# Retention attention feeding a gated MLP, on one core: scores of two heads on the two row halves of the PE array, and the running state kept as 64-column diagonal blocks

## The chip, the cores and the metric

The kernel runs on one core of a Trainium2 chip. The metric is the device time of one execution in microseconds (us); where several runs were made the median is given. "Granted clock" is the share of full TensorE clock that the throttle allowed. All profiles and ratios here are of fast runs; three of the 33 runs of the kernel before that stood beside the experiments were slow and are left out of the ratios.

Engines: PE multiplies matrices (PEld is its weight load, which overlaps), DVE is the vector engine, ACT the scalar engine, POOL the general one, SP issues the input DMAs.

## The reference, cut to what matters

```python
# q, k, v: (8 batches, 8 heads, 576 positions, 64), float32
scores = (q @ k.T) / sqrt(64)
ret = scores * Dmat              # Dmat[i, j] = gamma_h ** (i - j) for i >= j, else 0
x = (ret @ v)                    # heads side by side: (8, 576, 512)

h = gelu_tanh(x @ w_in)          # 512 -> 1024; u, v = its two halves
v_n = layer_norm(v) * g_ln
v_s = einsum('ts,bsd->btd', w_sg, v_n) + b_sg   # mixes positions
out = x + (u * v_s) @ w_out
```

## The kernel before

Two batches of 576 positions make nine tiles of 128 positions; four such periods make 36 tiles. The decay is folded into v and into a table, so a tile's attention is: scores with a triangular mask within the tile, plus a running state (64 x 64 per head) for everything earlier. Heads have 64 channels, so two heads fill 128 partitions. The kernel before multiplies a head pair at full array height by padding with zeros: `kbd` has the transposed k of one head in partitions 0 to 63 and zeros elsewhere, and so on; `zbd` is the state as a padded block-diagonal.

```python
    kbds = [consts.tile([128, KK, 2, 128], BF, ...) for i in range(2)]   # set to zero once
    zbds = [consts.tile([128, KK, 128], BF, ...) for i in range(2)]      # set to zero once

    def attn_T(i):            # transposes of k and q, and their way out of PSUM
        for a in (1, 0):
            for kk in range(KK):
                nc.tensor.transpose(tp[:, a, kk, :], s["qkb"][:, a, kk * 128:(kk + 1) * 128], ident[:])
        nc.scalar.activation(kbd[:64, :, 0, :], tp[:64, 1, :, :], Act.Copy)     # ACT: half of k
        nc.vector.tensor_copy(qT[:], tp[:, 0, :, :])                            # DVE: q
        nc.vector.tensor_copy(kbd[64:, :, 1, :], tp[64:, 1, :, :])              # DVE: other half of k

    def attn_S(i):            # scores, masked into ret
        for j in range(2):
            for r in range(4):
                kk, hh = 2 * j + r // 2, r % 2
                nc.tensor.matmul(sc[:, r, :], s["kbd"][:, kk, hh, :], s["qT"][:, kk, :], ...)
            nc.vector.tensor_tensor(ret[:, 4 * j:4 * j + 4, :], sc[:], msk..., op=Alu.mult)

    def attn_O(i):            # ot = state part + in-tile part; xT = ot * table
        ... nc.tensor.matmul(ot[r, kk, :n], st["zbd"][:, kk, r], s["qT"][:, kk, :n], ...)
        ... nc.tensor.matmul(ot[64 * hh:64 * hh + 64, kk, :], s["vp"][...], s["ret"][:, h, :], ...)
        nc.vector.tensor_tensor(xTs[p][...], ot[:], ttab[...], op=Alu.mult)

    def attn_Z(i):            # state update, and its copy for the next tile
        for kk in range(KK):
            nc.tensor.matmul(z[:, kk, :], kn[:, kk * 128:(kk + 1) * 128], s["vp"][:, kk * 128:(kk + 1) * 128], ...)
        nc.scalar.activation(zb[64:, :, 64:], z[64:, :, 64:], Act.Copy)         # ACT: half
        nc.vector.tensor_copy(zb[:64, :, 0:64], z[:64, :, 0:64])                # DVE: half

    for i in range(1, N + 1):           # ... loads, weight building and guards cut
        prep(i + 2)                     # POOL: casts of q, k, v
        attn_S(i)
        mlp_norm(i - 2)                 # ACT: vn = (vg - mean) * rstd
        run()                           # one queued unit: wp (mixing, then DVE gT) or op (output, then ACT ob)
        mlp_V(i - 1)                    # PE: hv; ACT: vg = gelu(hv)
        attn_T(i + 1)
        mlp_stats(i - 1)                # DVE: bst = bn_stats(vg)
        run()                           # another queued unit
        mlp_rstd(i - 1)                 # DVE: mv; POOL: rs, rs, nm
        mlp_U(i - 1)                    # PE: hu; ACT: uT
        attn_O(i); attn_Z(i)
```

So there are tiles with two wp units, tiles with two op units, and one tile per period with a single op unit (or none). They are called two-wp, two-op and one-op tiles below. The two-op tiles come in pairs; where one figure is given for them, it is that of the second of a pair.

## Time and profile before

| | before |
|---|---|
| time, median of 4 runs | 268.6 us (267.3 to 269.7) |
| span of the profiled execution, granted clock | 267.6 us, 0.973 |
| busy PE / DVE / ACT / POOL | 85 / 66 / 53 / 44% |
| tiles up to the start of the fifth xT | 46.1 us |
| the next 31 tiles (to the start of the last xT) | 199.2 us, 6.43 each |
| from there to the end | 22.3 us |

The first stage waits for DMA, the last is nearly all PE. (xT is the DVE product that ends a tile's attention; its start is a handy mark in the timeline.)

The first part of the page of the kernel before gives busy time, share and instructions of each engine:

```profile
PE 227.5 (85%) x2594; PEld 164.6 (62%) x2630; DVE 176.4 (66%) x394; ACT 143.1 (53%) x249; POOL 117.6 (44%) x202
```

The next lines are from its timeline: start, duration, engine, line, operation, outputs and inputs. They follow one loop through a tile with two op units; a bracket is idle time before the instruction and what ended it.

```profile
104.20 0.18 DVE L332 BATCH_NORM_AGGREGATE mv<-bst 128x2 f32<-128x6 f32 x1
...
105.82 0.82 ACT L349 ACTIVATE vn<-vg,nm,rs 128x512 bf16<-128x512 f32 x1 [1.46 <-POOL nm L337]
...
106.66 0.60 ACT L390 ACTIVATE ob<-op 128x512 f32<-128x512 f32 x1
...
107.67 0.60 ACT L322 ACTIVATE vg<-hv 128x512 f32<-128x512 f32 x1 [0.41 <-ACT ob L390]
108.16 0.58 ACT L254 ACTIVATE kbd_156<-tp 64x512 bf16<-64x512 bf16 x1
...
108.77 0.42 DVE L255 COPY qT<-tp 128x512 bf16<-128x512 bf16 x1 [2.15 <-ACT kbd_156 L254]
...
109.23 0.43 DVE L256 COPY kbd_156<-tp 64x512 bf16<-64x512 bf16 x1
...
109.69 0.69 DVE L327 BATCH_NORM_STATS2 bst<-vg 128x6 f32<-128x512 f32 x1
...
110.49 0.18 DVE L332 BATCH_NORM_AGGREGATE mv<-bst 128x2 f32<-128x6 f32 x1
```

Read it as a circle: the variance (mv) goes through three POOL steps (nm is the last; cut here) to the normalisation (vn) on ACT; ACT is in order, so ob, vg and the k copy stand behind vn; qT on DVE waits for ACT's k copy; the second half of k and bn_stats (bst) stand behind qT; then comes the next mv, 6.29 us after the first. That is exactly the time of a tile. PE in such a tile needs only 5.75 us (the sum of the distances between the starts of its groups), so it idles.

PE's groups for the attention, from the timeline of a tile with two wp units of the kernel before (x8 is the number of matmuls in the group; a group lasts until the next one starts):

```profile
122.90 0.41 PE L284 MATMUL ot<-qT,zbd_158 128*64 128x128 bf16 x8
123.15 0.39 PE L289 MATMUL ot<-ret,vsc_151 128*64 128x128 bf16 x8
123.47 0.40 PE L305 MATMUL zp<-vsc_151,qkb 128*128 128x128 bf16 x4
123.71 0.61 PE L267 MATMUL sc<-qT,kbd_156 128*128 128x128 bf16 x8
124.15 0.41 PE L372 MATMUL wp<-wT_0_178,vn 128*128 128x288 bf16 x2
```

From the first ot to wp is 1.25 us: state part 0.25, in-tile part 0.32, state update 0.24, scores 0.44.

### The profile page before, as it was taken

How to read it: one execution, taken by the hardware profiler on the slowest of the kernel's cores; microseconds unless marked ns; L12 is line 12 of the kernel's file. 1: busy time of each engine (PE TensorE's matmuls, PEld its weight loads, DVE VectorE, ACT ScalarE, POOL GpSimd, SP SyncE). 2: the span in 40 equal slices, each digit the busy share in tenths (PEclk: the TensorE clock that was granted, in tenths of full speed). 3: DMA queues.
4: the chain of work that ended last, by engine and by line, in shares of the span. 5: the costliest groups of instructions: out<-in, count | busy, mean ns of one | idle time of the engine just before them, and what ended most of it. 6: DMA issues, size and time to landing. Idle time of an engine off the chain costs nothing.

```text
span 267.6 us, 6555 instructions
## 1 busy us (share of the span) xinstructions
PE 227.5 (85%) x2594; PEld 164.6 (62%) x2630; DVE 176.4 (66%) x394; ACT 143.1 (53%) x249; POOL 117.6 (44%) x202
## 2 busy tenths in 40 slices
PE   0558669868999999969999999799999999799894
PEld 0337437646766776747766876468666766576552
DVE  4475667599856985568658866578669866575230
ACT  7274486763455446654465466624564466544513
POOL 7137642544455655535445444444446455311100
PEclk9999986999999999999999999979999999889999
DMA  8999996999527997599949968785683022000305
GB/s 150 247 283 202 273 271 148 226 212 220 99 81 198 194 218 181 163 248 182 199 134 223 219 144 212 186 155 107 142 218 80 2 80 81 39 2 0 133 26 196
DMA packets 120453, 42.64 MB, mean 159 GB/s; under 512 B 113700, under 2 KB 113700, under 8 KB 120424
## 3 DMA queue, kind: packets, MB, share of 16 engines
q1 hardware_dynamic: 114704, 32.79, 62.0%
q10 hardware_dynamic: 5720, 9.45, 9.8%
q8 instruction: 20, 0.33, 0.5%
q14 instruction: 9, 0.07, 0.1%
HBM read 32.80 MB, written 9.44 MB: 158 GB/s over the span
## 4 chain that ended last, share of the span: by engine, by line
PE 40%; DVE 19%; SPq 12%; ACT 10%; issue 8%; DMA 4%; POOL 4%; ACTq 2%; POOLq 0%; DVEq 0%
PE wp L372 13%; SPq L78 10%; PE hv L319 7%; PE hu L359 6%; DMA qk<-in_k_dram 4%; DVE bst L327 4%; DVE xT L292 3%; PE op L384 3%; ACT ob L390 3%; PE tp L251 3%; DVE qT L255 3%; DVE gT L377 3%; PE ot L284 2%; ACT kbd_155 L254 2%; ACT kbd_156 L254 2%
## 5 line engine op out<-in xcount | busy, mean ns | idle before, releaser
L255 DVE COPY qT<-tp 128x512 bf16<-128x512 bf16 x36 | 15.2, 424 | 60.0 <-ACT kbd_155 L254 35.3
L334 POOL TENSOR_SCALAR rs<-mv 128x1 f32<-128x1 f32 x36 | 8.0, 222 | 103.2 <-DVE mv L332 99.4
L349 ACT ACTIVATE vn<-vg,nm,rs 128x512 bf16<-128x512 f32 x32 | 26.0, 813 | 46.8 <-POOL nm L337 46.8
L238 POOL CAST qkb<-qk 128x1024 bf16<-128x1024 f32 x36 | 37.4, 1038 | 21.3 <-DMA qk<-in_k_dram 17.1
L319 PE MATMUL hv<-w_in,xT 128*128 128x512 bf16 x124 | 38.4, 407 | 4.4 <-DVE xT L292 2.2
L269 DVE TENSOR_TENSOR ret<-sc,tri 128x512 bf16<-128x512 f32 x64 | 40.7, 673 | 1.3 <-PE sc L267 1.3
L359 PE MATMUL hu<-xT,w_in 128*128 128x128 bf16 x576 | 39.4, 224 | 1.5 <-ACT wT_3_186 L227 1.5
L362 ACT ACTIVATE uT<-hu 128x512 bf16<-128x512 f32 x36 | 21.4, 596 | 31.2 <-PE hu L359 26.2
L359 PEld LDWEIGHTS <-w_in 128*128 128x128 bf16 x576 | 35.5, 100 | 2.4 <-issue 1.6
L384 PE MATMUL op<-w_out,gT 128*128 128x512 bf16 x128 | 34.7, 379 | 0.8
L251 PE MATMUL tp<-ident,qkb 128*128 128x128 bf16 x288 | 23.9, 231 | 9.7 <-POOL qkb L238 9.7
L372 PEld LDWEIGHTS <-vn 128*128 128x128 bf16 x256 | 24.9, 99 | 11.5 <-issue 5.7
L251 PEld LDWEIGHTS <-qkb 128*128 128x128 bf16 x288 | 20.2, 104 | 18.7 <-POOL qkb L238 10.9
L377 DVE TENSOR_TENSOR gT<-wp,uT 128x288 bf16<-128x288 f32 x64 | 26.0, 446 | 7.1 <-PE wp L372 6.5
L322 ACT ACTIVATE vg<-hv 128x512 f32<-128x512 f32 x36 | 21.5, 597 | 13.3 <-PE hv L319 6.3
L327 DVE BATCH_NORM_STATS2 bst<-vg 128x6 f32<-128x512 f32 x36 | 25.0, 694 | 3.9 <-ACT vg L322 2.8
L390 ACT ACTIVATE ob<-op 128x512 f32<-128x512 f32 x36 | 21.2, 590 | 9.2 <-PE op L387 8.4
L292 DVE TENSOR_TENSOR xT<-ot,ttab 128x512 bf16<-128x512 f32 x36 | 24.4, 679 | 2.0 <-PE ot L289 1.3
L319 PEld LDWEIGHTS <-xT 128*128 128x128 bf16 x144 | 13.0, 103 | 16.2 <-DVE xT L292 5.7
L335 POOL TENSOR_TENSOR rs<-rs,mhalf 128x1 f32<-128x1 f32 x36 | 20.4, 567 | 3.0
L384 PEld LDWEIGHTS <-gT 128*128 128x128 bf16 x144 | 12.6, 98 | 9.0 <-DVE gT L377 0.3
L267 PE MATMUL sc<-qT,kbd_156 128*128 128x128 bf16 x144 | 13.0, 225 | 5.7 <-ACT uT L362 2.4
(140 smaller groups left out, 377.0 us busy)
## 6 DMA issues: line engine op xcount, KB each, us to landing
out_dram<-ob ACTq DMA_DIRECT2D x36, 256.0 KB, 3.1
qk<-in_q_dram SPq DMA_DIRECT2D x32, 256.0 KB, 4.8
qk<-in_k_dram SPq DMA_DIRECT2D x32, 256.0 KB, 4.9
vf<-in_v_dram SPq DMA_DIRECT2D x32, 256.0 KB, 5.2
wst<-in_moe_w_in_dram SPq DMA_DIRECT2D x2, 1024.0 KB, 7.4
wst<-in_moe_w_sg_dram SPq DMA_DIRECT2D x1, 1152.0 KB, 7.3
qk<-in_q_dram SPq DMA_DIRECT2D x8, 128.0 KB, 4.5
qk<-in_k_dram SPq DMA_DIRECT2D x8, 128.0 KB, 4.5
```

The costliest lines, as they stand in the source:

```text
L78: nc.sync.dma_start(dst[p0:p0 + n], src[2 * p + b, :, r0:r0 + n, :].transpose([1, 0, 2]))
L238: nc.gpsimd.tensor_copy(qkb[:], qk[:].rearrange("p a h d -> p a (h d)"))
L251: nc.tensor.transpose(tp[:, a, kk, :], s["qkb"][:, a, kk * 128:(kk + 1) * 128], ident[:])
L269: nc.vector.tensor_tensor(ret[:, 4 * j:4 * j + 4, :], sc[:], msk[:].unsqueeze(1).to_broadcast([128, 4, 128]), op=Alu.mult)
L292: nc.vector.tensor_tensor(xTs[p][:, :, 128 * m:128 * m + 128], ot[:], ttab[:, :, t0:t0 + 128], op=Alu.mult)
L319: nc.tensor.matmul(hv[:], xTs[p][:, kk, 128 * m:128 * m + 128], w_in[:, kk, F2:], start=(kk == 0), stop=(kk == KK - 1))
L327: nc.vector.bn_stats(bst[:], vgs[i][0][:])
L359: nc.tensor.matmul(hu[:, c, :], w_in[:, kk, 128 * c:128 * c + 128], xTs[p][:, kk, 128 * m:128 * m + 128], start=(kk == 0), stop=(kk == KK ...
L372: nc.tensor.matmul(ps[half][:], vns[t0 + j][e][:, 128 * c:128 * c + 128], wT[e][j][:, half * HS:(half + 1) * HS], start=(j == 0), stop=(j ...
L377: nc.vector.tensor_tensor(gTs[p][:, c, col:col + HS], ps[half][:], uTs[p][:, c, col:col + HS], op=Alu.mult)
L384: nc.tensor.matmul(op[:], gTs[p][:, c, r], w_out[:, c, :], start=(c == 0), stop=False, skip_group_check=True)
L390: nc.scalar.activation(ob[:], op[:], Act.Copy)
```

## The change

Its intent: transpose k plainly and copy it once, whole, on ACT; let the two heads of a pair use the two row halves of the array at the same time; keep the state as 128 x 64 (two heads' 64 x 64 blocks below each other), again copied once. Two DVE copies per tile go, ACT's two copies keep their length (they have the same number of elements per partition), and no zeros are multiplied.

```diff
-        kbd = kbds[i % NK]
-        nc.scalar.activation(kbd[:64, :, 0, :], tp[:64, 1, :, :], Act.Copy)
+        kT = work.tile([128, KK, 128], BF, name="kT")
+        nc.scalar.activation(kT[:], tp[:, 1, :, :], Act.Copy)
         nc.vector.tensor_copy(qT[:], tp[:, 0, :, :])
-        nc.vector.tensor_copy(kbd[64:, :, 1, :], tp[64:, 1, :, :])
 ...
+        sc = [psS.tile([128, KK, 128], F32, name="sc", tag="sc") for _ in range(2)]
+        for kk in range(KK):
+            for hh in range(2):
+                r = slice(64 * hh, 64 * hh + 64)
+                nc.tensor.matmul(sc[hh][:, kk, :], s["kT"][r, kk, :], s["qT"][r, kk, :],
                                  start=True, stop=True, skip_group_check=True)
 ...
-                    nc.tensor.matmul(ot[r, kk, :n], st["zbd"][:, kk, r], s["qT"][:, kk, :n],
+                    nc.tensor.matmul(ot[r, kk, :n], st["zb"][r, kk, :], s["qT"][r, kk, :n],
 ...
-            nc.tensor.matmul(z[:, kk, :], kn[:, kk * 128:(kk + 1) * 128], s["vp"][:, kk * 128:(kk + 1) * 128],
-                             start=(kk == 0 and m in (0, MID)), stop=True, skip_group_check=True)
-        zb = zbds[i % NZ]
-        nc.scalar.activation(zb[64:, :, 64:], z[64:, :, 64:], Act.Copy)
-        nc.vector.tensor_copy(zb[:64, :, 0:64], z[:64, :, 0:64])
+            for hh in range(2):
+                c = slice(128 * kk + 64 * hh, 128 * kk + 64 * hh + 64)
+                nc.tensor.matmul(z[64 * hh:64 * hh + 64, kk, :], kn[:, c], s["vp"][:, c],
+                                 start=(kk == 0 and m in (0, MID)), stop=True, skip_group_check=True)
+        zb = work.tile([128, KK, 64], BF, name="zb")
+        nc.scalar.activation(zb[:], z[:], Act.Copy)
```

(Cut: the removed padded tiles and their memsets; ret's layout, now head half first; names.)

More of the change, by code (lines that the diff above doesn't have):

```diff
@@ L136 @@
         nc.scalar.activation(ttab[:, kk, :S], pos_f[:], Act.Exp, scale=lg_col[:, kk:kk + 1], bias=lsc[:])
-    NV, NK, NZ = 5, 2, 2
+    NV = 5
     vscs = [consts.tile([128, H * D], BF, name=f"vsc{i}") for i in range(NV)]
-    kbds = [consts.tile([128, KK, 2, 128], BF, name=f"kbd{i}") for i in range(NK)]
-    zbds = [consts.tile([128, KK, 128], BF, name=f"zbd{i}") for i in range(NZ)]
     kmid = consts.tile([128, H * D], BF, name="kmid")
     vmid = [[consts.tile([128, F2], BF, name=f"vmid{i}{e}") for e in range(2)] for i in range(2)]
-    for t in kbds + zbds:
-        nc.vector.memset(t[:], 0.0)
     for t in vmid:
@@ L252, in attn_T @@
         qT = work.tile([128, KK, 128], BF, name="qT")
-        kbd = kbds[i % NK]
-        nc.scalar.activation(kbd[:64, :, 0, :], tp[:64, 1, :, :], Act.Copy)
+        kT = work.tile([128, KK, 128], BF, name="kT")
+        nc.scalar.activation(kT[:], tp[:, 1, :, :], Act.Copy)
         nc.vector.tensor_copy(qT[:], tp[:, 0, :, :])
-        nc.vector.tensor_copy(kbd[64:, :, 1, :], tp[64:, 1, :, :])
-        s["qT"], s["kbd"] = qT, kbd
+        s["qT"], s["kT"] = qT, kT
     def attn_S(i):
@@ L261, in attn_S @@
         msk = tri_mid if i % NT == MID else tri
-        ret = work.tile([128, H, 128], BF, name="ret")
-        for j in range(2):
-            sc = psS.tile([128, 4, 128], F32, name="sc", tag="sc")
-            for r in range(4):
-                kk, hh = 2 * j + r // 2, r % 2
-                nc.tensor.matmul(sc[:, r, :], s["kbd"][:, kk, hh, :], s["qT"][:, kk, :],
+        ret = work.tile([128, 2, KK, 128], BF, name="ret")
+        sc = [psS.tile([128, KK, 128], F32, name="sc", tag="sc") for _ in range(2)]
[3 more added lines that the diff above has]
+                nc.tensor.matmul(sc[hh][:, kk, :], s["kT"][r, kk, :], s["qT"][r, kk, :],
                                  start=True, stop=True, skip_group_check=True)
-            nc.vector.tensor_tensor(ret[:, 4 * j:4 * j + 4, :], sc[:],
-                                    msk[:].unsqueeze(1).to_broadcast([128, 4, 128]), op=Alu.mult)
+        for hh in range(2):
+            nc.vector.tensor_tensor(ret[:, hh, :, :], sc[hh][:],
+                                    msk[:].unsqueeze(1).to_broadcast([128, KK, 128]), op=Alu.mult)
         s["ret"] = ret
@@ L288, in attn_O @@
                 h = 2 * kk + hh
-                nc.tensor.matmul(ot[64 * hh:64 * hh + 64, kk, :], s["vp"][:, 64 * h:64 * h + 64], s["ret"][:, h, :],
+                nc.tensor.matmul(ot[64 * hh:64 * hh + 64, kk, :], s["vp"][:, 64 * h:64 * h + 64], s["ret"][:, hh, kk, :],
                                  start=(m == 0 and kk == 0), stop=True, skip_group_check=True)
@@ L300, in attn_Z @@
         if m == 0 or m == MID:
-            zp[0] = psA.tile([128, KK, 128], F32, name="zp", tag="zp")
+            zp[0] = psA.tile([128, KK, 64], F32, name="zp", tag="zp")
         z = zp[0]
@@ L304, in attn_Z @@
         for kk in range(KK):
-            nc.tensor.matmul(z[:, kk, :], kn[:, kk * 128:(kk + 1) * 128], s["vp"][:, kk * 128:(kk + 1) * 128],
-                             start=(kk == 0 and m in (0, MID)), stop=True, skip_group_check=True)
-        zb = zbds[i % NZ]
-        nc.scalar.activation(zb[64:, :, 64:], z[64:, :, 64:], Act.Copy)
-        nc.vector.tensor_copy(zb[:64, :, 0:64], z[:64, :, 0:64])
-        st["zbd"] = zb
+            for hh in range(2):
+                c = slice(128 * kk + 64 * hh, 128 * kk + 64 * hh + 64)
[3 more added lines that the diff above has]
+        nc.scalar.activation(zb[:], z[:], Act.Copy)
+        st["zb"] = zb
     vns, vgs = {}, {}
```

## The prediction

> **What bounds the kernel now.** Three stages. (1) Up to about 48 us the chain of waits is DMA issue, then landings of q, k, v. (2) From 48 to 245 us, 31 tiles at some 6.3 us each (starts of the xT product in the timeline: 5.81 to 7.11 apart). (3) From 245 us the last output work, almost all PE, which the change does not touch. So only about 195 us can shrink.
>
> In stage 2 PE is nearly full but not the only limit. From starts in the timeline, PE needs 6.0 us in a tile with two spatial (wp) groups, 5.75 in one with two output (op) groups, 4.7 in one with one; over a nine-tile period about 51.3 us, against 57 elapsed. The 5.5 us of idle PE per period comes from a loop over ACT, DVE and POOL, plain in the timeline at 104 to 111 us: statistics (mv) -> three small POOL steps (1.4) -> ACT normalise (0.81) -> ob (0.60) -> its DMA issue (0.4) -> vg (0.5 until the next starts) -> k copy on ACT (0.58) -> DVE qT (0.42) -> DVE copy of the other half of k (0.43) -> bn_stats (0.70) -> mv; 6.29 us, as long as the tile. The waits view agrees: the normalisation waits 46.8 us for POOL.
>
> **What goes, comes and moves.**
> - DVE loses 36 k half copies (428 ns) and 32 state half copies (405 ns), 28 us of 176. ACT's two copies keep their free sizes, so their durations (580 and 378 ns). The k copy stands on that loop: with its start gap, 0.46 us less per tile. The state copy stands before ret and gT, which release PSUM for wp: up to 0.3 us more at one or two tiles of a period.
> - PE: eight score matmuls now take 0.45 us (56 ns each); in pairs on the row halves I estimate 0.25 to 0.30. State update: 4 x 56 = 0.23 us becomes eight 64-column matmuls; the half-width inter-chunk matmuls of the middle tile already run at about 18 ns each, so about 0.14.
> - Against it: the Trainium skill, "TensorEngine Tiling (Array Packing)", Key Properties, says that a change of tiling mode drains the engine. The trace agrees in size: the 16 hu matmuls need 0.90 us at their spacing, and the first half-column matmul starts 0.99 after them; going back costs 0.08. Mode changes go from two to four per tile: +0.18 us. Net PE per tile about -0.1, plus or minus 0.2.
>
> **On the critical path.** The loop falls from 6.29 to 5.83 us, where PE (5.75) nearly takes over; two-wp tiles are already PE-bound at 6.0 apart from stalls of 0.4 to 0.8 us, which shrink by 0.46 or more. I count 3.2 to 3.9 us per period, times 3.5 periods, about 11 to 13 us, plus 0.5 to 1 before 62 us; I take some off for PE taking over. Prediction 257 us (-4.2%), range 250.5 to 264. Faster 0.80, within 2% 0.17, slower 0.03.
>
> **What would show it.** DVE busy about 148 us; no wait of scores for k copies on DVE; the spacing of xT in two-op tiles 5.8 to 5.95 us; the PE gap before wp (0.66 at 120 us) down to about 0.2; first 45 us and last 20 us unchanged; groups ot, zp, sc together within 0.2 us of the 1.25 they take now.
>
> **What would make it wrong.** Mode changes between row-split, column-split and full use costing more than 0.1 us each, or row-half weight loads not overlapping, so that scores take 0.6 us or more: PE would eat the gain (same). Loads not keeping up at 5.9 us a tile. POOL or ACT queue order putting the wait back elsewhere. If PE shrinks more than I count, 251.

## The result, and the profile after

The kernel after takes 248.09 us (median of 4 runs, 247.23 to 248.34) against 268.6. The ratio is 0.9232, 95% interval 0.9185 to 0.9280. A ratio here is the mean time of one kernel's fast runs over that of the other's fast runs of the same rounds, so it is not quite the ratio of the medians. The forecast was 257 us, range 250.5 to 264: the direction was right and the gain nearly twice what was said.

| stage (profiled executions) | before | after |
|---|---|---|
| to the fifth xT | 46.1 us | 45.8 us |
| next 31 tiles | 199.2 us | 178.4 us |
| to the end | 22.3 us | 22.4 us |

All of the gain is in the 31 tiles: 0.67 us per tile on average. Starts of xT are the measure: the second two-op tile of a pair went from 6.29 to 5.63 us (the first from 6.29 to 5.27 in one pair and from 6.39 to 5.52 in the other), the one-op tile from 7.1 to 6.3, the longest of the two-wp tiles from 6.4 to 5.9. The first nine-tile period after the two early tiles took 56.8 us before and 51.7 after.

```profile
PE 215.9 (88%) x2758; PEld 155.0 (63%) x2758; DVE 144.6 (59%) x322; ACT 140.7 (57%) x249; POOL 118.4 (48%) x202
```

The part of the page above is again busy time, now of the kernel after: DVE lost 31.8 us. The same loop in its timeline, a two-op tile at the same place:

```profile
97.94 0.18 DVE L329 BATCH_NORM_AGGREGATE mv<-bst 128x2 f32<-128x6 f32 x1
...
99.56 0.81 ACT L346 ACTIVATE vn<-vg,nm,rs 128x512 bf16<-128x512 f32 x1 [0.73 <-POOL nm L334]
...
100.28 0.58 ACT L387 ACTIVATE ob<-op 128x512 f32<-128x512 f32 x1
...
101.33 0.60 ACT L319 ACTIVATE vg<-hv 128x512 f32<-128x512 f32 x1 [0.47 <-PE tp L246]
...
101.83 0.59 ACT L249 ACTIVATE kT<-tp 128x512 bf16<-128x512 bf16 x1
...
102.45 0.42 DVE L250 COPY qT<-tp 128x512 bf16<-128x512 bf16 x1 [2.24 <-ACT kT L249]
102.79 0.68 DVE L324 BATCH_NORM_STATS2 bst<-vg 128x6 f32<-128x512 f32 x1
...
103.58 0.18 DVE L329 BATCH_NORM_AGGREGATE mv<-bst 128x2 f32<-128x6 f32 x1
```

The circle is 5.64 us now, 0.65 shorter, although the copy that went took only 0.43. Step by step, from start to start:

| step | before | after |
|---|---|---|
| mv to nm | 1.32 | 1.33 |
| nm to vn | 0.30 | 0.29 |
| vn to ob | 0.84 | **0.72** |
| ob to vg | 1.01 | 1.05 |
| vg to the k copy, to qT | 1.10 | 1.12 |
| qT to the half copy of k | 0.46 | gone |
| the instruction in front, to bst | 0.46 | **0.34** |
| bst to mv | 0.80 | 0.79 |
| sum | 6.29 | 5.64 |

Besides the copy and its start gap (0.46), two other starts came 0.12 us sooner each, though nothing in those instructions was changed. The circle takes 5.62 to 5.66 us in the two-op tiles of the two periods looked at, also where the starts of xT are 5.25 or 5.52 us apart, so this is the loop's own length and not that of PE's work.

PE's groups for the attention after, again in a tile with two wp units:

```profile
114.99 0.41 PE L280 MATMUL ot<-qT,zb 64*64 64x128 bf16 x8
115.33 0.41 PE L285 MATMUL ot<-ret,vsc 128*64 128x128 bf16 x8
115.58 0.29 PE L303 MATMUL zp<-vsc,qkb 128*64 128x64 bf16 x8
115.80 0.40 PE L262 MATMUL sc<-qT,kT 64*128 64x128 bf16 x8
116.13 1.15 PE L369 MATMUL wp<-wT,vn 128*128 128x288 bf16 x8
```

From the first ot to wp is 1.14 us: state part 0.34 (with a change of array mode behind it), in-tile part 0.25, update 0.22, scores 0.33 (again with a mode change). That is 0.11 less than before, as forecast. In the two-op tile PE's groups now add up to 5.62 us with no gap: PE and the loop end together.

One more difference was not foreseen at all. Before, the three tiles that follow a one-op tile took 5.81, 6.96 and 6.91 us; after, 5.51 or 5.52. The windows view of the kernel before (stretch; its length; busy time and instruction count of PE, PEld, DVE, ACT, POOL; granted clock; DMA share; GB/s) shows why:

```profile
174.00:176.00 2.00, 2.00 (x14) 1.32 (x12) 1.87 (x5) 0.00 (x0) 1.08 (x4) 0.60 1.32 206
176.00:178.00 2.00, 1.78 (x9) 0.84 (x8) 1.54 (x4) 0.82 (x2) 1.96 (x2) 0.54 0.08 10
```

At 174 to 178 us the granted clock is 0.54 to 0.60, following a stall of PE before the scores:

```profile
173.16 0.22 PE L267 MATMUL sc<-qT,kbd_156 128*128 128x128 bf16 x1 [1.64 <-ACT uT L362]
...
174.27 0.54 PE L372 MATMUL wp<-wT_1_179,vn 128*128 128x288 bf16 x2
...
175.08 0.69 PE L372 MATMUL wp<-wT_3_181,vn 128*128 128x288 bf16 x2
```

The pair of wp matmuls at 175.08 is followed by the next 0.48 us later, twice the 0.245 of the undisturbed tile. After, the same stall is 0.95 us (before the scores at 160.97 us), and the clock stays up:

```profile
163.00:165.00 2.00, 1.92 (x18) 1.27 (x17) 1.30 (x3) 1.76 (x3) 2.00 (x3) 1.00 0.66 124
```

Against the one that was spared, the two slow tiles cost 1.15 and 1.1 us; so some 2.2 of the 20.8 us came from a clock that no longer drops in these tiles. Not every such stall dropped it: the one before 116.36 us, as long as the others, did not. Over the profiles of all runs, the one-op tiles have 21 stalls of 1.6 to 2.2 us before the scores, and a lowered clock follows 13 of them; they have 12 of 0.7 to 1.0 us, and it follows none. The times agree: of the 30 fast runs of the kernel before that stood beside the experiments, the six with the highest mean clock (0.984) took 265.3 to 267.2 us, the six with the lowest (0.965 and 0.966) 267.7 to 270.5. (In the first stage both kernels show a clock of 0.50 from about 38 to 44 us; that is outside the 31 tiles.)

### The profile page after: what moved, and what is told of

Same layout as the page of the kernel before. It is cut to its first block, busy times and chain, and to the rows that moved or that the text cites. A ratio compares the mean times of both kernels' runs of the same rounds, so it can differ in the third digit from the quotient of the medians.

```text
span 246.6 us, 6787 instructions
## 1 busy us (share of the span) xinstructions
PE 215.9 (88%) x2758; PEld 155.0 (63%) x2758; DVE 144.6 (59%) x322; ACT 140.7 (57%) x249; POOL 118.4 (48%) x202
## 4 chain that ended last, share of the span: by engine, by line
PE 49%; DVE 12%; ACT 9%; SPq 9%; DMA 8%; issue 6%; POOL 5%; ACTq 1%; POOLq 0%; DVEq 0%
PE wp L369 12%; PE op L381 10%; PE hu L356 8%; SPq L78 8%; PE hv L316 6%; DMA qk<-in_k_dram 5%; DVE ret L265 3%; PE tp L246 3%; PE ot L285 3%; DVE gT L374 3%; DVE bst L324 2%; ACT kT L249 2%; PE op L384 2%; PE ot L280 2%; PE sc L262 2%
## 5 line engine op out<-in xcount | busy, mean ns | idle before, releaser
L250 DVE COPY qT<-tp 128x512 bf16<-128x512 bf16 x36 | 15.3, 424 | 66.9 <-ACT kT L249 66.9
L235 POOL TENSOR_TENSOR vsc<-vf,gv 128x512 bf16<-128x512 f32 x36 | 37.8, 1050 | 1.5 <-DMA vf<-in_v_dram 1.2
L369 PE MATMUL wp<-wT,vn 128*128 128x288 bf16 x256 | 37.4, 286 | 0.6 <-ACT vg L319 0.3
L381 PE MATMUL op<-w_out,gT 128*128 128x512 bf16 x144 | 37.1, 380 | 0.0
L369 PEld LDWEIGHTS <-vn 128*128 128x128 bf16 x256 | 24.2, 98 | 10.4 <-issue 3.5
L249 ACT ACTIVATE kT<-tp 128x512 bf16<-128x512 bf16 x36 | 21.3, 592 | 2.0 <-PE tp L246 1.9
L262 PE MATMUL sc<-qT,kT 64*128 64x128 bf16 x288 | 14.7, 223 | 8.8 <-ACT uT L359 5.6
```

The costliest lines, as they stand in the source:

```text
L235: nc.gpsimd.tensor_tensor(vp[:].rearrange("p (h d) -> p h d", h=H), vf[:], gv[:, m, :].unsqueeze(2).to_broadcast([128, H, D]), op=Alu.mult)
L249: nc.scalar.activation(kT[:], tp[:, 1, :, :], Act.Copy)
L369: nc.tensor.matmul(ps[half][:], vns[t0 + j][e][:, 128 * c:128 * c + 128], wT[e][j][:, half * HS:(half + 1) * HS], start=(j == 0), stop=(j ...
L381: nc.tensor.matmul(op[:], gTs[p][:, c, r], w_out[:, c, :], start=(c == 0), stop=False, skip_group_check=True)
```

## The experiments

Theories at the start. **L**: the loop over ACT, DVE and POOL is nearly everything, and a copy that starts at partition 64 costs its neighbours more than its own time. **P**: the loop gave only the forecast 0.46 us, and the surprise lies in PE's shorter groups. All runs are timed beside runs of the kernel before; the first two of the three batches ran on one chip and the third on another, so medians of different batches compare only to about a microsecond, and ratios to the kernel before are the safer measure.

| run | what | time, us | ratio to before, 95% interval |
|---|---|---|---|
| b_nodve | before, DVE copies left out (wrong result) | 250.71 | 0.9333 (0.9287 to 0.9379) |
| a_kz | after, DVE copies put back as dummies | 263.62 | 0.9819 (0.9775 to 0.9863) |
| a_k64 | after, one dummy at partitions 64 to 127 | 262.89 | 0.9786 (0.9750 to 0.9822) |
| a_k0 | after, the same dummy at 0 to 63 | 256.21 | 0.9544 (0.9500 to 0.9588) |
| m_scores | scores half of the change alone | 251.35 | 0.9386 (0.9328 to 0.9444) |
| m_state | state half alone | 266.75 | 0.9961 (0.9899 to 1.0023) |
| a_unpair | after, score order changed | 247.63 | 0.9255 (0.9199 to 0.9310) |
| a_kdve | after, k copied on DVE | 243.28 | 0.9074 (0.9025 to 0.9124) |
| b_swapz | before, state halves exchanged | 267.77 | 1.0010 (0.9959 to 1.0062) |
| b_swapkz | before, halves of state and k exchanged | 263.33 | 0.9856 (0.9803 to 0.9908) |
| a_onehalf | after, all scores on one row half (wrong result) | 251.55 | 0.9424 (0.9378 to 0.9469) |
| c_3modes | a_kdve with the state padded again | 244.74 | 0.9158 (0.9115 to 0.9200) |

### DVE's share and PE's share: b_nodve and a_kz

```diff
 # b_nodve, from before
-        nc.vector.tensor_copy(kbd[64:, :, 1, :], tp[64:, 1, :, :])
-        nc.vector.tensor_copy(zb[:64, :, 0:64], z[:64, :, 0:64])
 # a_kz, from after
         nc.vector.tensor_copy(qT[:], tp[:, 0, :, :])
+        nc.vector.tensor_copy(scratch[64:], tp[64:, 1, :, :])
 ...
         nc.scalar.activation(zb[:], z[:], Act.Copy)
+        nc.vector.tensor_copy(scratch[:64, :, 0:64], z[:64, :, :])
```

> The kernel before without its two DVE half copies (wrong result on purpose: half of each head pair's keys and states stay zero); PE instructions exactly as before. Theory L (the loop over ACT, DVE and POOL was nearly all of it, and losing a copy that starts at partition 64 frees more than its 0.46 us): the loop falls to about 5.7, PE at 5.75 takes over in two-output tiles; 250 to 253 us. Rival P (the loop gives only the 0.46 us forecast, and the rest of the 20 us comes from the shorter PE groups): 256 to 259 us.

> The kernel after with two DVE copies of the old sizes put back at the old places, into a scratch tile that nobody reads; PE as after. Theory L: the loop is back at about 6.2 us, the shorter PE groups gain next to nothing; 261 to 266 us. Rival P: the shorter PE groups keep their gain; 255 to 259 us.

Measured: 250.71 and 263.62 us. Both lie where L put them and outside P. With PE exactly as before, losing the two copies is worth 6.7%; with PE as after and the copies back, 1.8% is left. Together they make a square: the kernel before 268.5, copies out 250.7, PE changed 263.6, both 248.1. Most of the gain is the copies, and once they are out, the new PE groups add 1% (0.9333 to 0.9232). In b_nodve the two-op tiles take 5.72 to 5.82 us, near PE's own old time of 5.75, so there PE is the bound. The square is not quite clean: in a_kz ACT's state copy also starts at partition 0, so that ob follows vn after 0.72 us instead of 0.84, and its two-op tiles take 6.14 us as in b_swapz below, where PE is as before. So the 1.8% is not PE alone.

### What one copy costs depends on where it starts: a_k64 and a_k0

```diff
 # a_k64, from after (a_k0: [:64] in place of [64:])
         nc.vector.tensor_copy(qT[:], tp[:, 0, :, :])
+        nc.vector.tensor_copy(scratch[64:], tp[64:, 1, :, :])
```

> The kernel after with only the k half copy (partitions 64 to 127) put back on DVE as a dummy. Theory L: loop 5.64 + 0.46 + 0.12 = 6.2 us in two-output tiles, 259 to 263 us; the gap between the starts of qT and that copy and of that copy and bn_stats is 0.46 each. Theory C (only the copy's own time counts, wherever it starts): the same time as the next run.

> As the run before, but the dummy copies the half at partitions 0 to 63: same size, start partition as its neighbours'. Theory L with the hold at a change of start partition: starts 0.34 apart instead of 0.46, loop about 6.0 us, 4 to 6 us faster than the run before: 254 to 258 us. Theory C: within 1 us of the run before.

Measured: 262.89 and 256.21 us, 6.7 us apart (no overlap of the six runs of each), for a copy of the same shape and nearly the same duration; theory C falls. The two timelines, first a_k64, then a_k0:

```profile
105.47 0.42 DVE L251 COPY qT<-tp 128x512 bf16<-128x512 bf16 x1 [2.44 <-ACT kT L250]
...
105.92 0.43 DVE L252 COPY scratch<-tp 64x512 bf16<-64x512 bf16 x1
...
106.36 0.69 DVE L326 BATCH_NORM_STATS2 bst<-vg 128x6 f32<-128x512 f32 x1
```

```profile
103.73 0.42 DVE L251 COPY qT<-tp 128x512 bf16<-128x512 bf16 x1 [2.56 <-ACT kT L250]
104.07 0.41 DVE L252 COPY scratch<-tp 64x512 bf16<-64x512 bf16 x1
104.40 0.68 DVE L326 BATCH_NORM_STATS2 bst<-vg 128x6 f32<-128x512 f32 x1
```

With the copy at 64, starts are 0.45 and 0.44 us apart; with the copy at 0, 0.34 and 0.33: an instruction then starts about 0.08 us before the one in front has ended. The two-op tiles take 6.20 and 5.96 us. The Trainium skill, "VectorE: DVE Perf Modes", section "Two Vector instructions with no wait between them", describes this: "A held instruction starts only when every earlier Vector instruction has finished", and an instruction is held where its input or output starts in another 32-partition quadrant than the last one's. The trace agrees, and gives the price on this chip: about 0.12 us each time, twice per copy, since the next instruction must change back.

### Which half of the change: m_scores and m_state

```diff
 # m_scores: the after kernel with zbd, the 128-column update and both half copies of the state as before
 # m_state: the before kernel with zb, the diagonal-block update and the one state copy as after
```

> The scores half of the change alone (k copied whole on ACT, scores on row halves), the state as before. Theory L: the k copy leaves the loop with its two holds (0.58 us), the hold before ob on ACT stays, loop 5.75; the state copy on DVE stays before ret and gT; PE group ot, zp, sc about 1.25 - 0.12 + 0.1; 251 to 254 us. Rival P: half of the gain, 257 to 259 us.

> The state half of the change alone (diagonal blocks, state copy whole on ACT), scores as before. Theory L: the k copy and its holds stay on the loop (only the 0.12 us hold of ob goes): 6.17 us per two-output tile, and the state copy no longer delays ret and gT; 261 to 265 us. Rival P: half of the gain, 257 to 259 us.

Measured: 251.35 us, in its range, and 266.75 us, slower than its range. The k copy is what mattered; the state copy is beside the loop. The two-op tiles of m_state take 6.20 to 6.22 us, near the 6.17 that L gave. L missed two things there. A period without a lowered clock hardly shrank (the tiles up to the one-op tile took 56.1 us against 56.8), since the one-op tile grew from 7.11 to 7.17 and the two-wp tiles gave back only 0.1 to 0.2 each. And the clock: the tiles after the one-op tile take 6.77, 6.94 and 6.92 us, with the clock down in all three places (0.94 over the three stretches of 29 us that hold them; in the first, 0.63 and 0.51 in the two worst 2 us), since the stall in front of them stayed, 1.78 us. In the one profile of m_state that is one drop more than in that of before, about 1 us; it does not account for the whole miss.

### Exchanging halves, with no other change: b_swapz and b_swapkz

```diff
 # b_swapz, from before; b_swapkz exchanges the halves of k in the same way as well
-        nc.scalar.activation(zb[64:, :, 64:], z[64:, :, 64:], Act.Copy)
-        nc.vector.tensor_copy(zb[:64, :, 0:64], z[:64, :, 0:64])
+        nc.scalar.activation(zb[:64, :, 0:64], z[:64, :, 0:64], Act.Copy)
+        nc.vector.tensor_copy(zb[64:, :, 64:], z[64:, :, 64:])
```

> The kernel before with the halves of the state copy exchanged: ACT copies partitions 0 to 63, DVE 64 to 127; the same instructions and sizes, a correct result. If ACT too holds an instruction whose start partition differs from the last one's, ob no longer waits for the end of the normalisation (0.72 instead of 0.84 between their starts): 0.12 us off the loop in two-output tiles, 265 to 267 us. If start partitions do not matter on ACT: within 1 us of before.

> The kernel before with the halves of both copies exchanged, k and state; the same instructions and sizes, a correct result. With the hold at changed start partitions: on DVE qT, k half and bn_stats follow at 0.34 instead of 0.46 (two times 0.12 saved), on ACT ob is freed (0.12) but the k half is now held behind vg (0.11 lost): loop 6.29 - 0.25 = 6.04, 261 to 264 us. If only durations matter: within 1 us of before.

Measured: 267.77 us (no change) and 263.33 us (1.4% faster). The second is in its range: a correct kernel with the same instructions, sizes and order of engines gains 1.4% from which half each engine takes; its two-op tiles take 6.02 to 6.08 us, against 6.04 forecast. The first missed in total time and hit in mechanism. From its timeline:

```profile
103.45 0.69 DVE L292 TENSOR_TENSOR xT<-ot,ttab 128x512 bf16<-128x512 f32 x1
...
104.17 0.43 DVE L309 CAST zbd<-zp 64x256 bf16<-64x256 f32 x1
...
104.63 1.29 DVE L269 TENSOR_TENSOR ret<-sc,tri 128x512 bf16<-128x512 f32 x2
...
104.85 0.81 ACT L349 ACTIVATE vn<-vg,nm,rs 128x512 bf16<-128x512 f32 x1 [1.60 <-POOL nm L337]
...
105.57 0.58 ACT L390 ACTIVATE ob<-op 128x512 f32<-128x512 f32 x1
```

On ACT, ob follows vn after 0.72 us instead of 0.84, so ACT too starts an instruction early only if its start partition fits; and the two-op tiles fell from 6.29 to between 6.14 and 6.22. But the DVE copy now starts at 64: from xT to it 0.72 instead of 0.61, from it to ret 0.46 instead of 0.33. In two-wp tiles gT and wp stand behind ret, and one such tile in each period went from 5.82 us to 6.02. Most of what was won in one kind of tile was paid in the other: the first full period took 56.6 us against 56.8.

### What PE gains from row halves: a_unpair and a_onehalf

```diff
 # a_unpair, from after
-        for kk in range(KK):
-            for hh in range(2):
+        for hh in range(2):
+            for kk in range(KK):
 # a_onehalf, from after: both heads read partitions 0 to 63
-                nc.tensor.matmul(sc[hh][:, kk, :], s["kT"][r, kk, :], s["qT"][r, kk, :],
+                nc.tensor.matmul(sc[hh][:, kk, :], s["kT"][:64, kk, :], s["qT"][:64, kk, :],
```

> The kernel after with its scores in the order head half outer, pair inner, so that neighbouring score matmuls use the same row half. If row halves run at once only when neighbours differ: the eight take about 0.45 us instead of about 0.25, PE per tile +0.2, and since PE is now busy all through the tiles the time rises by nearly 31 x 0.2 = 6 us, to 252 to 255 us. If pairing gives nothing, or PE has slack: within 1 us of the kernel after.

> The kernel after with all eight score matmuls reading partitions 0 to 63 (wrong result on purpose), so that both heads use the same row half. If the two row halves run at once, whatever the program order: one half must now do all eight, 8 x 56 ns = 0.45 instead of about 0.22, PE per tile +0.22 us, and as PE is the bound 252 to 255 us. If a row-half matmul of 128 columns takes half the time by itself: within 1 us of the kernel after (248).

Measured: 247.63 us for a_unpair, no change, against the forecast of 252 to 255. The order of the eight matmuls does not matter, although the program as built does have four of one half and then four of the other: they still start within 0.19 us, two at a time (0.18 in the kernel after). a_onehalf took 251.55 us, just below its range. Its scores:

```profile
104.96 0.62 PE L262 MATMUL sc<-qT,kT 64*128 64x128 bf16 x8
105.73 0.59 PE L381 MATMUL op<-w_out,gT 128*128 128x512 bf16 x2 [0.16 <-issue]
```

The group shows 0.62 us where it showed 0.40 with both halves: eight starts over 0.40 us instead of 0.18. So a single row half is no faster per matmul than the full array (0.057 us for 128 columns), and the gain is that both halves work at once. The Trainium skill, "TensorE: Matmul & The Clock Gate", section "Why this matters for your kernels", says the same of small contractions ("gain is tile concurrency"). The longest two-wp tiles took 6.12 us against 5.90, the expected 0.22; the one-op tile, which stalls anyway, gave 0.3 back.

### Beyond the change: a_kdve and c_3modes

The kernel after still has qT waiting for ACT's k copy (66.9 us of DVE's idle time in the waits view), while DVE has room.

```diff
 # a_kdve, from after
-        nc.scalar.activation(kT[:], tp[:, 1, :, :], Act.Copy)
+        nc.vector.tensor_copy(kT[:], tp[:, 1, :, :])
 # c_3modes, from a_kdve: the state padded to block-diagonal again
-                    nc.tensor.matmul(ot[r, kk, :n], st["zb"][r, kk, :], s["qT"][r, kk, :n],
+                    nc.tensor.matmul(ot[r, kk, :n], st["zbd"][:, kk, r], s["qT"][:, kk, :n],
 ...
-        nc.scalar.activation(zb[:], z[:], Act.Copy)
+        nc.scalar.activation(zb[:64, :, 0:64], z[:64, :, :], Act.Copy)
+        nc.vector.tensor_copy(zb[64:, :, 64:], z[64:, :, :])
```

> The kernel after with the whole k copy on DVE instead of ACT. DVE loses its wait for ACT (66.9 us of idle time before qT); the loop loses the k copy's wait on ACT. PE is the bound in eight tiles of nine, so only the stall in the one-output tile (about 1 us per period of nine) and in the weight-building tiles can go: 243 to 247 us. If the extra 15 us on DVE delay ret and gT: 248 to 251.

> The kernel after with k copied on DVE (243.3 us) and with the state kept in a zero-padded block-diagonal tile (two half copies, ACT 0 to 63, DVE 64 to 127), so that the inter-chunk matmuls use the column-half mode of their neighbours: three mode changes per tile instead of four. If a mode change costs 0.08 to 0.1 us of PE: the step from the first ot group to the second falls from 0.34 to 0.24, PE per tile -0.1, 240 to 242 us. If the change between two half-size modes is free or DVE's extra copy comes onto the critical path: 243 to 246.

Measured: a_kdve 243.28 us, in its range and faster than both kernels. Its one-op tile takes 4.67 us instead of 6.3 (PE's own time by the prediction's count, 4.7); the other eight of a period together are within 0.3 us of the kernel after. The chain of waits (shares of the span by engine) says what is left; first after, then a_kdve:

```profile
PE 49%; DVE 12%; ACT 9%; SPq 9%; DMA 8%; issue 6%; POOL 5%; ACTq 1%; POOLq 0%; DVEq 0%
```

```profile
PE 77%; SPq 8%; DVE 5%; ACT 3%; DMA 2%; POOL 2%; issue 1%; DVEq 0%; POOLq 0%
```

c_3modes took 244.74 us, outside the 240 to 242 of its first alternative, inside the 243 to 246 of its second, and if anything slower than a_kdve (the intervals of the two ratios overlap, from different batches and chips). From its timeline:

```profile
103.11 0.41 PE L283 MATMUL ot<-qT,zbd 128*64 128x128 bf16 x8
103.35 0.39 PE L288 MATMUL ot<-ret,vsc 128*64 128x128 bf16 x8
...
111.73 1.38 PE L373 MATMUL wp<-wT,vn 128*128 128x288 bf16 x8 [0.48 <-DVE gT L378]
```

The mode change is indeed gone: from the state part to the in-tile part 0.24 us, against 0.34 after; two-op tiles take 5.50 us instead of 5.62. The same 0.1 us shows in the middle tile of a period, whose state part has half the columns (0.14 to 0.15 us against 0.24 to 0.25), so it is a fixed cost and not that of slower matmuls. So a change of array mode costs about 0.1 us of PE, also between two part-array modes. But two-wp tiles went from 5.90 to 6.02, with the stall that the last line shows: PE waits for gT, which stands behind a DVE copy at partition 64 and a held ret. The second alternative of the expectation is what happened.

## Why the prediction was wrong

- **Where the gain would come from: right.** First 46 and last 22 us unchanged; DVE lost the copies; no score waits for a DVE k copy; the loop was the bound in two-op tiles, and PE took over.
- **The failed step: "with its start gap, 0.46 us less per tile", and so "the loop falls from 6.29 to 5.83 us, where PE (5.75) nearly takes over".** The loop fell by 0.65 to 5.64. The copy's own term was right (0.46), but its effect on neighbours was left out: bst starts 0.12 us sooner behind qT, ob 0.12 sooner behind vn, because instructions that start at partition 64 no longer stand among instructions that start at 0. So the term of the loop should have been 0.65 (0.70 less 0.05 of small differences). a_k64 against a_k0 shows it for DVE (6.7 us in all), b_swapz and b_swapkz for ACT and for the kernel before. I read the start gaps in the trace as fixed overhead; comparing pairs of instructions with and without a change of partition would have shown that they are not.
- **"Net PE per tile about -0.1": right in size (0.11), and undercounted in the sum.** With the loop at 5.83 it would have been hidden in most tiles; with the loop at 5.64 every tile but one per period became PE-bound and it counted. The runs with and without the copies put it at 1% of the time.
- **"Mode changes go from two to four per tile: +0.18 us": in line with what was measured.** One of them is 0.1 us in c_3modes; the others were not taken apart. The Trainium skill, "TensorEngine Tiling (Array Packing)", Key Properties, names the drain but no size for it. Scores cost 0.33 us with their mode change, in line with the estimate for the bare group (0.25 to 0.30) plus that change.
- **Left out: the clock.** In the profile before, two tiles of 31 ran at a lowered clock after a PE stall (about 2.2 us in all); with the shorter loop that stall is 0.95 us, a length after which no profile here shows a lowered clock. The windows view showed 0.97 there, and I read it as harmless.
- **Sum.** I counted 11 to 13 us plus 0.5 to 1 in the early tiles, then took some off. Measured in the tiles: 20.8 us. Of these 16.3 are the loop and PE in ordinary tiles (5.1 to 5.3 us in a period instead of the 3.2 to 3.9 counted), 2.2 are the clock's, and 2.2 fell in the two early tiles where ACT also builds weights. That early part is not settled: one of its two tiles differs between the profiles by 1.7 us, in part because POOL got to its statistics later after a late input DMA (its cast started at 45.0 against 44.0 us), and a_kz, with DVE loaded as before, got through that stage as early as the kernel after.

What stays open: why the state copy dummy of a_kz left its two-op tiles slightly faster (6.14 us) than a_k64's (6.20), and what decides whether a stall of 1.6 to 2.2 us drops the clock.

## What to carry to other kernels

Before costing an engine's instruction that covers half the partitions, look at the start gaps around it: taking it away, or giving the halves to the engines so that neighbours start at the same partition, can be worth a further quarter of its duration on each side (here 0.12 us beside a copy of 0.43). When a loop over several engines and the matmul engine are within a few per cent of each other, cost both to 0.05 us, since a small gain on either counts only once the other has gone below it. And a short stall of PE is worth more than its length if it lowers the clock for the next microseconds.

## What the Trainium skill lacked or had wrong

- "VectorE: DVE Perf Modes", section "Two Vector instructions with no wait between them", has the rule for held instructions but no price: here 0.12 us per held start (0.46 against 0.34 us between starts, copies of 128 x 512 and 64 x 512), twice per odd instruction, and 6.7 us of a 256 us kernel.
- The section speaks of the vector engine alone, and I found nothing of it on the pages on ScalarE: here ACT shows the same, ob 0.84 us after vn where the last PSUM read had started at partition 64, 0.72 us where it had started at 0 (before against b_swapz).
- "TensorEngine Tiling (Array Packing)", Key Properties, says that a mode change drains the engine, without a figure: here about 0.1 us, between the full array and column halves and between two part-array modes (0.34 against 0.24 us for the same eight matmuls in the kernel after and c_3modes).
- "TensorE: Matmul & The Clock Gate", section "Why this matters for your kernels", advises against PE gaps over about 3 us between bursts: here gaps of 1.6 us, interrupted by one matmul and followed by 0.25 us more, were followed by a clock of 0.54 to 0.61 for some 4 us in two of three cases in the kernel before, and stalls of 1.6 to 2.2 us by a lowered clock in 13 of 21 cases over all profiles.
- The same page, Part 3, says that matmuls start in strict program order: in a_unpair, as built, four matmuls of one row half stand in front of the four of the other, and all eight still start within 0.19 us, two at a time, about as in the interleaved order, where a single half needs 0.40. The profile does not say which started when, and no run here shows whether a later step of compilation changed the order, so how they overlap, and whether the page is wrong, is not shown.
